# The column form of w by small TensorE products, with the issue order drawn up anew, in a fused linear-attention and feed-forward kernel

## The chip, the cores and the metric

One core of one Trainium2 chip. The metric is the device time of one execution in microseconds (us). Engines are named as the profile names them: PE is TensorE (PEld its weight loads), DVE is VectorE, ACT is ScalarE, POOL is GpSimd, SP is the queue of SyncE that issues most transfers. SBUF and PSUM are the two on-chip memories in which the kernel's tiles lie; the results of PE come into PSUM (`bank` in the profile). A *point* is 1% of the time of the kernel before.

## The reference, cut to what matters

```python
# r, k, v: (batch 4, heads 8, seq 768, head_dim 48); w, u: (8, 48)
state = zeros((B, H, D, D))
for t in range(S):
    cur = einsum('bhd,bhe->bhde', u * k[t], v[t])
    y[t] = einsum('bhd,bhde->bhe', r[t], state + cur)
    state = w[:, :, None] * state + einsum('bhd,bhe->bhde', k[t], v[t])
x = y.transpose(0, 2, 1, 3).reshape(3072, 384)
h = maximum(x @ w_in, 0)          # w_in  (384, 2048)
out = (h * h) @ w_out             # w_out (2048, 384)
```

The kernel works on 24 units, each 128 tokens of one batch. Inside a unit the recurrence becomes products of r and k with powers of w, a masked 128x128 product, and a state handed to the next unit of the same batch, which is scaled by w to the power 128. That last factor is wanted with the head dimension along the partitions: this is the "column form" of w.

## The kernel before

The kernel is a list of steps in one string, `ORDER`, and a table of functions, `Do`. A step such as `P0.10:D/0` says: product P0 of unit 10, on DVE, into buffer 0. The letter after the colon is the engine (A ACT, D DVE, G POOL, P PE, S the SP queue). Each engine runs its steps in the order of the string, so the string decides both which engine does a step and what stands ahead of it. The steps that matter here:

```python
def wc(e):                       # w as a column, by a transfer of single values
    for h in range(2):
        e.dma_start(out=wcol[64 * h : 64 * h + D, :], in_=w.rearrange("(a e) d -> e d a", e=2)[h])
def WLcol(e):                    # its 128th power
    e.activation(wcol, wcol, AF.Ln)
    e.activation(wcol, wcol, AF.Exp, scale=float(L))
def WLm(e): ...                  # spread to (128, 4, 96): factor of the state
def kh(e, i): e.tensor_mul(rk[..][:, 1, :, 0:D], loaded("k", i), early("WkP") if i < EARLY else Wkhat)
def rh(e, i): e.tensor_mul(rk[..][:, 0, :, 0:D], loaded("r", i), early("WtP") if i < EARLY else Wt2)
def P0(e, i): e.tensor_mul(P0b[..], loaded("r", i), loaded("k", i))
def P1(e, i): e.tensor_mul(t, t, ub)                       # t is P0b of the unit
def du(e, i): e.tensor_reduce(dub[..], P0b[..], axis=X, op=ALU.add)
def dv(e, i): e.tensor_mul(dvb[..], loaded("v", i), t)     # t is du, spread
def S(e, i):  e.tensor_mul(S0W[i % B], tsb[..], WLm)
# ... T, X: transposes by PE; Tc, xTc: their copies out of PSUM; XB, xX: the same by DMA
# ... A, Bm, Y, U, xs, ts: the attention; F1, re, sq, F2, os, out: the feed-forward part
# ... Z: PE products that nobody reads; cW: casts of weights; vb: cast of v
for step in ORDER.split():
    ...
    getattr(Do, name)(E[eng[0]], *at, *map(int, eng[1:]))
```

The six products kh, rh, P0, P1, dv and S have both inputs in SBUF (for the first four units kh and rh take one from PSUM). Each can run on DVE or on POOL, and the order says which, unit by unit.

## Time and profile before

| | before |
|---|---|
| time, median of 3 runs | 179.08 us (178.46 to 180.28) |
| span of the profiled execution | 178.6 us, mean granted clock 0.990 |
| PE, DVE, POOL busy | 166.0, 146.4, 58.8 us |
| PE idle (span less busy) | 12.6 us |

PE is the engine to watch: its idle time is the only thing that an order can win or lose, apart from the work itself. The groups of instructions by shape: here are three of VectorE's; the columns are line, engine, operation, tile and inputs, shapes, count, then busy us, mean ns of one, and idle time before them:

```profile
L342 DVE TENSOR_TENSOR P<-ldr,ldk 128x384 f32<-128x384 f32 x19 | 11.4, 606 | 0.0
L354 DVE TENSOR_TENSOR dv<-ldv,du 128x384 f32<-128x384 f32 x13 | 7.1, 550 | 0.0
L424 DVE TENSOR_TENSOR S0W<-ts,WLm 128x384 bf16<-128x384 f32 x11 | 6.6, 600 | 0.0
```

And two that have one input in PSUM (bank):

```profile
L411 DVE TENSOR_TENSOR xs<-bank,dv 128x384 bf16<-128x384 f32 x24 | 13.1, 551 | 2.1 <-POOL dv L354 1.8
L421 DVE TENSOR_TENSOR ts<-bank,S0W 128x384 f32<-128x384 f32 x16 | 8.8, 547 | 1.8 <-PE bank L403 1.8
```

The same shape, with both inputs in SBUF, takes 550 ns in one row and 606 in another. I use one sum for this all through the document, and call it **DVE's excess**: over all of DVE's TENSOR_TENSOR groups whose inputs are both in SBUF, count x (mean - 550 ns), with 415 ns in place of 550 for the bf16 squares (hq<-hr). For the kernel before it is 6.3 us.

### The profile page before, as it was taken

The numbers are of one execution on the slowest core, as the hardware profiler recorded it, in microseconds if no ns is written. First come the engines' busy times: TensorE is split into PE (matmuls) and PEld (weight loads), VectorE is DVE, ScalarE is ACT, GpSimd is POOL, SyncE is SP. The second block draws the span as 40 slices with busy tenths as digits, with TensorE's granted clock in tenths as the row PEclk, the third lists the DMA queues.
The fourth block names the chain that finished last, engine by engine and source line by source line (L and its number), as shares of the span: only waits on it lengthen the run. The fifth ranks groups of instructions, "written<-read, shape, count | busy, mean of one in ns | idle before, by whom it ended". The sixth has DMA issues, their size and how long they took to land.

```text
span 178.6 us, 4501 instructions
## 1 busy us (share of the span) xinstructions
PE 166.0 (93%) x1764; PEld 127.2 (71%) x1764; DVE 146.4 (82%) x294; ACT 108.6 (61%) x199; POOL 58.8 (33%) x70
## 2 busy tenths in 40 slices
PE   4986999989999979999989997999999999999992
PEld 4964987756788757776757665777768777877750
DVE  4999888595999999999999968999799659666420
ACT  2475875846597976978747655857835545332601
POOL 4084491036364533283377350292050000000000
PEclk9999699999999999999999999999999999999999
DMA  5998999989799999999999999997981200402122
GB/s 109 215 231 261 306 191 188 200 170 218 144 206 236 178 204 215 209 203 158 220 224 85 225 208 184 199 165 184 229 84 44 48 0 21 158 3 88 44 101 79
DMA packets 103749, 28.72 MB, mean 161 GB/s; under 512 B 96296, under 2 KB 103728, under 8 KB 103728
## 3 DMA queue, kind: packets, MB, share of 16 engines
q1 hardware_dynamic: 101688, 26.26, 73.9%
q0 software_dynamic: 1744, 1.77, 6.1%
q10 hardware_dynamic: 296, 0.40, 0.6%
q8 instruction: 14, 0.23, 0.5%
q14 instruction: 7, 0.06, 0.1%
HBM read 20.46 MB, written 4.72 MB: 141 GB/s over the span
## 4 chain that ended last, share of the span: by engine, by line
PE 42%; DVE 33%; DMA 14%; issue 5%; POOL 3%; ACT 1%; SPq 1%; DVEq 0%; POOLq 0%
PE bank L472 21%; PE bank L445 16%; DVE Bm L384 8%; DMA W<-in_moe_w_out_dram 6%; DMA wsa<-in_moe_w_in_dram 4%; DVE P L342 3%; DVE xs L411 3%; DVE du L349 3%; DVE rk L336 3%; DVE S0W L424 2%; DVE rk L339 2%; DVE ts L421 2%; DVE P L346 2%; DMA ldr<-in_r_dram 2%; POOL W L333 2%
## 5 line engine op out<-in xcount | busy, mean ns | idle before, releaser
L445 PE MATMUL bank<-xT,W 128*128 128x256 bf16 (+1 forms) x624 | 75.7, 268 | 1.8 <-DVE hq L462 1.1
L472 PE MATMUL bank<-W,hq 128*128 128x384 bf16 x384 | 72.0, 326 | 0.8 <-DMA W<-in_moe_w_out_dram 0.8
L445 PEld LDWEIGHTS <-W 128*128 128x128 bf16 x624 | 56.9, 100 | 13.1 <-issue 1.9
L453 ACT ACTIVATE hr<-bank 128x512 bf16<-128x512 f32 x76 | 44.4, 598 | 28.0 <-PE bank L445 27.2
L472 PEld LDWEIGHTS <-hq 128*128 128x128 bf16 x384 | 36.3, 98 | 19.6 <-issue 1.0
L460 ACT ACTIVATE hq<-hr 128x512 bf16<-128x512 bf16 x57 | 34.2, 628 | 4.4 <-DVE hr L455 4.2
L384 DVE TENSOR_TENSOR Bm<-bank,maskJT 128x512 bf16<-128x512 f32 x48 | 31.4, 681 | 2.2 <-PE bank L376 2.2
L260 ACT COPY os<-bank 128x384 f32<-128x384 f32 x18 | 8.6, 478 | 18.0 <-PE bank L472 16.0
L464 DVE TENSOR_TENSOR hq<-hr 128x512 bf16<-128x512 bf16 x37 | 15.3, 435 | 5.0 <-ACT hr L453 4.8
L455 DVE TENSOR_SCALAR hr<-bank 128x512 bf16<-128x512 f32 x20 | 13.8, 690 | 6.0 <-PE bank L445 4.5
L346 POOL TENSOR_TENSOR P<-P,ub 128x384 f32<-128x384 f32 x11 | 11.8, 1077 | 15.1 <-DVE P L342 15.0
L336 POOL TENSOR_TENSOR rk<-ldk,Wkhat 128x384 bf16<-128x384 f32 x9 | 10.8, 1205 | 13.2 <-DMA ldk<-in_k_dram 8.8
L354 POOL TENSOR_TENSOR dv<-ldv,du 128x384 f32<-128x384 f32 x11 | 9.1, 829 | 18.1 <-DVE du L349 15.0
L411 DVE TENSOR_TENSOR xs<-bank,dv 128x384 bf16<-128x384 f32 x24 | 13.1, 551 | 2.1 <-POOL dv L354 1.8
L394 PE MATMUL bank<-vb,Bm 128*128 128x48 bf16 x192 | 11.5, 184 | 2.4 <-DVE Bm L384 2.4
L349 DVE TENSOR_REDUCE du<-P 128x8 f32<-128x384 f32 x24 | 13.0, 542 | 0.1
L394 PEld LDWEIGHTS <-Bm 128*128 128x128 bf16 x192 | 9.6, 96 | 3.7 <-DVE Bm L384 2.3
L481 PE MATMUL bank<-identity 128*128 128x128 bf16 x101 | 9.7, 268 | 2.3 <-POOL identity masks.py:199 2.3
L342 DVE TENSOR_TENSOR P<-ldr,ldk 128x384 f32<-128x384 f32 x19 | 11.4, 606 | 0.0
L260 ACT COPY rkT<-bank 128x1024 bf16<-128x1024 bf16 x9 | 9.1, 1014 | 2.7 <-PE bank L363 2.6
L339 POOL TENSOR_TENSOR rk<-ldr,Wt 128x384 bf16<-128x384 f32 x6 | 7.1, 1183 | 9.6 <-DMA ldr<-in_r_dram 9.6
L481 PEld LDWEIGHTS <-identity 128*128 128x128 bf16 x101 | 8.3, 124 | 2.7 <-POOL identity masks.py:199 2.3
(62 smaller groups left out, 168.7 us busy)
## 6 DMA issues: line engine op xcount, KB each, us to landing
ldr<-in_r_dram SPq DMA_DIRECT2D x24, 192.0 KB, 3.8
ldk<-in_k_dram SPq DMA_DIRECT2D x24, 192.0 KB, 3.8
ldv<-in_v_dram SPq DMA_DIRECT2D x24, 192.0 KB, 3.9
out_dram<-os SPq DMA_DIRECT2D x22, 192.0 KB, 2.2
wsa<-in_moe_w_in_dram SPq DMA_DIRECT2D x7, 384.0 KB, 5.8
W<-in_moe_w_out_dram POOLq DMA_DIRECT2D x4, 384.0 KB, 8.8
out_dram<-os ACTq DMA_DIRECT2D x2, 192.0 KB, 1.9
rkT<-rk SPq DMA_TRANSPOSE x15, 3.7
```

Source lines behind the costliest of these rows:

```text
L260: e.copy(o, a)
L336: e.tensor_mul(rk[slot[f"rk{i}"]][:, 1, :, 0:D], loaded("k", i), early("WkP") if i < EARLY else Wkhat)
L342: e.tensor_mul(P0b[slot[f"P{i}"]], loaded("r", i), loaded("k", i))
L349: e.tensor_reduce(dub[slot[f"dv{i}"]], P0b[slot[f"P{i}"]], axis=mybir.AxisListType.X, op=ALU.add)
L384: e.tensor_mul(Bmb[slot[f"Bm{i}{h}"]], heads(bank(f"bA{i}{h}"), 128), mask_b)
L394: e.matmul(y[:, hc, D * h : D * (h + 1)], m[h][:, hc, :], vb[:, 2 * hc + h, :], start=(c == 0), stop=True, skip_group_check=True,)
L411: e.tensor_add(xsb[slot[f"xs{i}"]].rearrange("p (a b) -> p a b", a=HP), heads(bank(f"bY{i}"), 2 * D), dvb[slot[f"dv{i}"]].rearrange("p (a ...
L445: e.matmul(hp[:, fi, :], W1[f // 2][:, c, 128 * (f % 2) : 128 * (f % 2 + 1)], xt[:, c, :], start=(c == 0), stop=(c == CCH - 1), skip_group ...
L453: e.activation(hr, hp, AF.Relu)
L460: e.activation(hq, hr, AF.Square)
L472: e.matmul(bank(f"bO{i}", "bO")[:, 0:d_model], hqb[slot[f"hq{g},{f // m}"]][:, at : at + L], W2[q][:, f % 4, :], start=(f == 0), stop=(f = ...
L481: e.matmul(banks[b][:, 0:128], identity, identity, start=True, stop=True, skip_group_check=True)
```

## The change

Its intent: the two transfers of 4-byte values, which lie on a full DMA queue, go; eight PE products of one row by a 1x1 one turn the row of w, which is already in SBUF, into the column; and the issue order is drawn up anew around this.

```diff
-    nc.vector.memset(wcol, 1.0)
+    one = const.tile([1, 1], FP32, name="one")
+    nc.vector.memset(one, 1.0)
...
         def wc(e):
-            for h in range(2):
-                e.dma_start(out=wcol[64 * h : 64 * h + D, :], in_=w.rearrange("(a e) d -> e d a", e=2)[h])
+            for h in range(H):
+                p0 = 64 * (h % 2)
+                e.matmul(
+                    bank("bW")[p0 : p0 + D, h // 2 : h // 2 + 1], wb[0:1, h, :], one,
+                    start=True, stop=True, skip_group_check=True,
+                )
 
         def WLcol(e):
-            e.activation(wcol, wcol, AF.Ln)
-            e.activation(wcol, wcol, AF.Exp, scale=float(L))
+            for p0 in (0, 64):
+                e.activation(wcol[p0 : p0 + D, :], bank("bW")[p0 : p0 + D, 0:HP], AF.Ln)
+                e.activation(wcol[p0 : p0 + D, :], wcol[p0 : p0 + D, :], AF.Exp, scale=float(L))
...
 ORDER = """     (all lines replaced; two of them, with products that changed engine)
-Y.8:P/2 P1.10:D ... rh.11:D X.9:P/3 ... S.7:D sq.4.3:A0/25 ... S.6:D os.5:A/0
+P0.10:G/1 F1.4.0:P/0 ... rh.11:G re.4.3:A/3 ... S.6:G ... P1.10:G ... S.7:G
```

For units 4 and later, 63 of the steps P0, P1, kh, rh, dv, S and vb changed engine, in both directions. Of the 51 products with both inputs in SBUF that POOL now does for these units, 33 were DVE's before; of the 41 that it did before, 23 went to DVE.

## The prediction

> **What bounds the kernel now.** I first read the page's busy shares and its slices, to find the regimes.
>
> ```profile
> PE 166.0 (93%) x1764; PEld 127.2 (71%) x1764; DVE 146.4 (82%) x294; ACT 108.6 (61%) x199; POOL 58.8 (33%) x70
> ...
> PEclk9999699999999999999999999999999999999999
> DMA  5998999989799999999999999997981200402122
> ```
>
> TensorE (PE) is busy 93% of 178.6 us, the sixteen DMA engines are full until about 125 us, and the granted TensorE clock dips in one slice near 20 us. Next came a table of stretches (columns: stretch, length, busy time and count of PE, PEld, DVE, ACT, POOL, granted clock, DMA share, GB/s), to see which engine is full where:
>
> ```profile
> 16.00:18.00 2.00, 1.00 (x24) 0.75 (x22) 2.00 (x4) 0.85 (x2) 0.54 (x1) 1.00 0.93 283
> 18.00:20.00 2.00, 1.83 (x22) 1.66 (x20) 1.90 (x5) 1.42 (x2) 0.00 (x0) 0.60 1.16 317
> 20.00:22.00 2.00, 2.00 (x23) 2.00 (x22) 1.49 (x4) 1.86 (x5) 1.61 (x2) 0.55 1.14 289
> ...
> 60.00:80.00 20.00, 18.87 (x216) 14.38 (x215) 19.97 (x36) 15.89 (x31) 9.87 (x10) 1.00 1.02 207
> 80.00:100.00 20.00, 19.32 (x204) 13.91 (x202) 19.89 (x39) 13.09 (x26) 11.25 (x11) 1.00 1.20 178
> ...
> 100.00:120.00 20.00, 18.52 (x199) 13.74 (x198) 17.50 (x35) 13.67 (x27) 7.83 (x8) 1.00 1.02 198
> 120.00:140.00 20.00, 20.00 (x219) 15.22 (x217) 18.77 (x39) 11.70 (x22) 4.07 (x5) 1.00 0.63 122
> ```
>
> There are four regimes. Until 18.6 us PE waits for data and does little that counts. From there to 37 us it is nearly always busy, and waits for the second weight matrix at the end. From 44 to about 104 us VectorE (DVE) has no idle time and PE only little. From 110 us PE alone sets the end. The chain of waits in order of time, and the timeline, show the joints:
>
> ```profile
> 13.58 6.73 DMA wsa<-in_moe_w_in_dram
> 20.36 0.81 POOL W L262
> ...
> 25.25 0.69 POOL W L333
> 25.95 11.37 DMA W<-in_moe_w_out_dram
> ...
> 167.91 7.16 PE bank L472 x44
> 175.09 0.48 ACT os L260
> ```
>
> The reader should see that the transfer of column w is nowhere in it: the chain passes from the weights' loads through the POOL queue to the last load of w_out. What the transfer cost is in the view of its tile:
>
> ```profile
> L305 SPq DMA_DIRECT2D wcol<-in_w_dram x2: 438/462/486, 20.3 to 20.8; - x2
> L314 POOL COPY WLm<-wcol x2: 337/343/349, 28.1 to 28.5; 48x192 f32<-48x192 f32 x2
> ...
>   POOL WLm L314: 1.4, 1
> ...
>   DVE S0W L418: 0.3, 1
> ...
> DMA to landing us min/median/max: 4.4/4.4/4.4
> ```
>
> Two issues of 0.46 us on the SP queue, landing 4.4 us later; POOL waited 1.4 us and DVE 0.3 us for what is made of it.
>
> My budget of PE time: the span is 18.6 us until the first product with w_in, then work to 175.1, then 3.5 us of last copy and store. PE's gaps after 25 us, summed from the table of stretches, are 0.2 (25 to 30) + 0.8 (35 to 40) + 1.1 + 0.7 + 1.5 (60 to 120) = 4.3 us. Clock: 0.40 x 2.0 + 0.45 x 2.0 = 1.7 us of PE's full-clock time is withheld between 18 and 22 us. So if everything else stayed, no order of issue could win more than about 6 us, and a 2% gain (3.6 us) needs more than half of that.
>
> **What the Trainium skill says.** "TensorE: Matmul & The Clock Gate", section "What's actually happening": the gate opens after a busy window of some 3.4 us and falls to half rate after an idle one. The trace agrees in size (0.55 to 0.60 over 18 to 22 us, after a stretch with PE busy 1.00 of 2.00 us), though PE was not wholly idle before it. "DMA: Bandwidth & Descriptors", section "Specifications": under 512 B a transfer is not at line rate; the page's DMA line has 96296 of 103749 packets under 512 B, and the engines are full at some 200 GB/s. The 4-byte values of w are the extreme of that, but there are only 2 x 48 x 4 = 384 of them, 0.4% of the packets. "SBUF — State Buffer", section "Who interferes with whom": a VectorE instruction with two SBUF inputs contends with a GpSimd one that reads SBUF. The trace agrees: the product for rk from r takes 548 ns on DVE while its factor is in PSUM (4 early ones) and 629 ns with both in SBUF (14 later ones).
>
> **The change, part by part.** (a) Removed: two SP issues (0.97 us of SP time), 384 packets. At 73.9% of 16 engines' 178.6 us for 101688 packets a packet costs some 21 ns of one engine, so an estimate of 384 x 21 / 16 = 0.5 us of the DMA's time in the full stretch. Worth 0 to 0.5 us.
>
> (b) Added: eight products of one row by one column, 48 results each, after the first unit's transposes, where PE has filler work anyway; an estimate of 8 x 0.1 to 0.2 us = 0.8 to 1.6 us there if each is split in several passes, none of it on the later path. ScalarE runs four small functions rather than two, 4 x 0.2 = 0.8 us, before 12 us, where it has gaps. WLm is then ready on POOL near 19 us rather than 28.85. The state products S0 follow at once, but DVE lost only 0.3 us there.
>
> (c) The start. ScalarE now loads its table (1.28 us) before it issues the load of the row of w, rather than after. In the trace the issue begins at 1.37 and the data land 2.99 us later; it will now begin near 2.2, so every step made from w shifts by some 0.8 us. Against that stand weights: w_in's first slice is the 14th load on SP in both orders behind the same bytes (ten loads of r, k, v, two slices), landed at 17.6 us, and must be cast (0.9 us). I count the new DVE order from the shuffle to the second unit's xs: some 24 instructions of about 0.5 us, which gives the first w_in product 18.6 to 19.4 rather than 18.6. A loss of 0 to 0.8 us.
>
> (d) Fillers. Z products go from 101 to 127: 61 rather than 50 at the start, then 66 rather than 51 between the early steps, with 25 and 18 placed in the gaps of 11 to 17 us. I take it that the dip at 18 to 22 us goes, or mostly: 0 to 1.7 us won, which more than pays for (c).
>
> (e) POOL's queue. W.1.3, the last w_out load, was issued at 26.0 us after a cast (0.82 us) among the issues. That cast moves to DVE, and WLm's copies come ahead. By the POOL order the five issues start near 21.0 rather than 22.0 and end near 24.7. Those loads share full DMA engines, so I credit 0.5 to 1 us of landing, 36.5 rather than 37.35.
>
> (f) Moves between engines, counted from the two orders, each at the mean of its row in the groups by shape. Off DVE: 5 P0 (606), 3 S (600), 3 dv (550), 4 os (554), 6 rh (629), 3 squares in bf16 (435), 3 vb (349) = 3.0 + 1.8 + 1.7 + 2.2 + 3.8 + 1.3 + 1.0 = 14.8 us. Onto DVE: 2 P1 (666), 3 kh (675), 2 re (690), 2 squares from PSUM (680), 3 Tc (no DVE row; an estimate of 0.9 us from 357 ns for 384 columns), 2 casts of weights (estimate 0.7 from 349 ns for half), 3 xTc (357) = 1.3 + 2.0 + 1.4 + 1.4 + 2.7 + 1.4 + 1.1 = 11.3 us. DVE has 3.5 us less, near 143. POOL gets 10 us more (5 P0, 6 rh, 3 S, 3 dv; less 3 kh, 2 P1, 2 casts, 1 vb), near 69, and will lengthen DVE's two-input instructions by an estimated 1 us. Of the 2.5 us net, PE can gain at most what it idles for want of DVE, part of the 3.3 us between 60 and 120: say 1 us.
>
> (g) Two more units transposed by PE rather than by DMA: 6 products of 0.11 us = 0.7 us on PE, which is the bound. Two DMA transposes less lie on the full SP queue.
>
> Sum, middle values: (a) -0.2, (b) 0, (c) +0.4, (d) -0.9, (e) -0.5, (f) -1.0, (g) +0.7 = -1.5 us. (d) and (e) overlap, since PE that runs ahead then waits for w_out. From 179.1 that is 177.6.
>
> **The rivals.** First, the transfer was hidden and nothing takes its place: the SP queue and DMA are full with other loads, PE goes on at 93%, gaps move about. For: the chain of waits leaves wcol out. That gives 178.5 to 179.5. Second, a new wait: GpSimd takes rh, P0, S and dv at 0.8 to 1.2 us each, some double of DVE's, and these stand ahead of transposes and xs; if POOL is late, DVE and PE wait, as already at 106.3 us, where xs waited 1.8 us for dv on POOL. Against: POOL is at 33%. That would give 180 to 182. Third, the late w: unit 0 and 1 come late, F1 starts at 20 us and the clock still falls: 179.5 to 181. Fourth, all gains arrive and the new order also closes half the gaps of 60 to 120 us: 175 to 176.
>
> **Range and chances.** I give my sum 50%, the first rival 22%, the second and third together 15%, the fourth 13%. Median 177.6 us, 175.5 to 180.0 eight times in ten. 2% faster means below 175.5 us, where only the fourth gets to: 0.12. 2% slower means above 182.7: 0.04.
>
> **What would show it.** Right: the clock above 0.9 in 18 to 22 us; the shuffle of w near 5.3 us rather than 4.5; WLm done near 20 us; the last w_out load landed before 37 us; DVE near 143, POOL near 69; w_in's first product at 18.6 to 19.4 us; PE full from 110 us on. Wrong: the clock falls again, PE's gaps after 25 us add up to over 5 us, or waits of DVE for POOL over 2 us each. A result below 175 would mean that gaps of DVE and PE were closed that I left standing; one above 181, that POOL or the late row of w set a new bound.

## The result, and the profile after

| | before, same rounds | after |
|---|---|---|
| time, median | 178.77 us (178.22 to 180.28) | 188.81 us (187.92 to 189.6) |
| ratio of the fast runs, 95% interval | | 1.0546 (1.0464 to 1.0628) |
| span of the profiled execution | 178.6 us | 187.2 us |
| PE busy, idle | 166.0, 12.6 us | 168.1, 19.1 us |
| DVE's excess | 6.3 us | 17.9 us |

A ratio is the mean time of one kernel's fast runs over the mean of the other's fast runs in the same rounds, so it is not quite the ratio of the two medians.

The change is slower by 5.5%. The prediction of 177.6 us, with its range to 180.0, was wrong. The page of the kernel after:

```profile
PE 168.1 (90%) x1812; PEld 127.9 (68%) x1812; DVE 154.2 (82%) x284; ACT 108.5 (58%) x204; POOL 70.9 (38%) x79
...
PEclk9999999999988999999999999999999999999999
```

DVE does ten instructions fewer and is busy 7.8 us longer. The dip of the granted clock at 20 us is gone, but there is one two slices wide at 51 to 61 us. In the table of stretches of the kernel after (columns: stretch, length, busy time and count of PE, PEld, DVE, ACT, POOL, clock, DMA share, GB/s):

```profile
18.00:20.00 2.00, 2.00 (x43) 1.90 (x39) 1.73 (x4) 1.65 (x4) 1.88 (x5) 1.00 0.89 274
20.00:22.00 2.00, 2.00 (x46) 1.93 (x43) 2.00 (x5) 2.00 (x4) 2.00 (x4) 1.00 0.98 299
50.00:60.00 10.00, 7.23 (x74) 4.94 (x73) 8.58 (x15) 5.12 (x11) 3.12 (x3) 0.83 1.05 166
80.00:100.00 20.00, 17.50 (x198) 13.14 (x195) 19.22 (x32) 11.68 (x24) 8.86 (x9) 1.00 0.72 151
100.00:120.00 20.00, 18.26 (x193) 13.74 (x188) 19.80 (x34) 13.45 (x28) 11.31 (x11) 1.00 0.86 177
120.00:140.00 20.00, 18.38 (x207) 13.89 (x205) 19.27 (x35) 12.77 (x25) 9.75 (x9) 1.00 0.71 145
```

and the one row of the same view of the kernel before that the prediction left out:

```profile
50.00:60.00 10.00, 10.00 (x126) 8.16 (x123) 9.97 (x20) 8.90 (x18) 5.05 (x6) 1.00 1.03 205
```

The loss stands in these rows. PE idles 2.77 + 2.50 + 1.74 + 1.62 = 8.6 us in 50 to 60 and 80 to 140 us; before it was 0 + 0.68 + 1.48 + 0 = 2.2 us. The difference of 6.4 us is as much as the whole growth of PE's idle time (19.1 - 12.6 = 6.5); what else changed, 1.8 us more from 22 to 25 us and less in other stretches, cancels out. In the remaining 2.1 us of the span PE is busy longer. It does 48 instructions more (26 products Z, 16 for w and 6 transposes), but that these are the 2.1 us is not shown: runs told below with the same 1812 instructions were busy between 163.8 and 168.1 us. In 100 to 140 us DVE is busy 39.1 of 40 us and still does fewer instructions than before (69 rather than 74). So DVE's instructions have become longer. And it is DVE that PE waits for. Of the 8.6 us, 8.4 end with an instruction of DVE by the view of waits, and none with one of POOL; here are those of 50 to 60 and of 80 to 100 us (who waited for whom, us, times, longest):

```profile
PE bank L382 <- DVE rkT L263: 1.5, 1, 1.5
PE bank L382 <- DVE ts L427: 1.2, 1, 1.2
...
PE bank L398 <- DVE Bm L390: 1.8, 1, 1.8
PE bank L409 <- DVE Bm L390: 0.7, 1, 0.7
```

The groups by shape of the kernel after, to be laid beside those of before:

```profile
L348 DVE TENSOR_TENSOR P<-ldr,ldk 128x384 f32<-128x384 f32 x14 | 11.3, 810 | 0.0
L360 DVE TENSOR_TENSOR dv<-ldv,du 128x384 f32<-128x384 f32 x10 | 7.9, 792 | 0.0
L430 DVE TENSOR_TENSOR S0W<-ts,WLm 128x384 bf16<-128x384 f32 x8 | 7.7, 963 | 0.0
...
L417 DVE TENSOR_TENSOR xs<-bank,dv 128x384 bf16<-128x384 f32 x24 | 13.0, 550 | 2.0 <-PE bank L400 1.7 <-POOL dv L360 0.3
L427 DVE TENSOR_TENSOR ts<-bank,S0W 128x384 f32<-128x384 f32 x16 | 8.7, 546 | 0.4 <-POOL S0W L430 0.4
```

606 to 810, 550 to 792 and 600 to 963 ns, for the same operation on the same shapes. The last two rows, with one input in PSUM, kept their length (551 to 550 and 547 to 546 ns). Instruction by instruction the trace says the same. In the kernel after, 40 of DVE's 103 two-input instructions overlap in time with a product, cast or copy of POOL, and they hold all of the excess, 17.9 us, some 0.45 us each and at most 0.83; the other 63 hold 0.0. In the kernel before it is 27 of 118 with 6.3 us, some 0.23 each, and 91 with 0.0. The timeline of the kernel after shows where the first gap comes from (columns: start, length, engine, line, operation, tile and inputs, count, and in brackets the idle time before it and what ended it):

```profile
46.04 2.44 POOL L342 TENSOR_TENSOR rk<-ldk,Wkhat 128x384 bf16<-128x384 f32 x2 [0.91 <-PE bank L400]
...
47.55 2.62 DVE L348 TENSOR_TENSOR P<-ldr,ldk 128x384 f32<-128x384 f32 x2
...
48.44 1.31 POOL L345 TENSOR_TENSOR rk<-ldr,Wt 128x384 bf16<-128x384 f32 x1
...
49.71 1.31 POOL L348 TENSOR_TENSOR P<-ldr,ldk 128x384 f32<-128x384 f32 x1
50.09 1.35 DVE L352 TENSOR_TENSOR P<-P,ub 128x384 f32<-128x384 f32 x1
...
52.54 0.38 PE L382 MATMUL bank<-rkT 48*128 48x128 bf16 x7 [1.23 <-DVE ts L427]
...
53.74 0.68 DVE L263 COPY rkT<-bank 128x1024 bf16<-128x1024 bf16 x1
...
54.47 0.61 PE L382 MATMUL bank<-rkT 48*128 48x128 bf16 x8 [1.55 <-DVE rkT L263]
```

From 47.55 to 51.44 us DVE does three products, which would take 3 x 0.55 = 1.65 us, and needs 3.89, while POOL works through four of its own without a pause, from 46.04 to 51.02 us. The copy rkT, which PE waits for, stands behind them in DVE's queue, and behind one more product that took 0.94 us. PE works 0.61 us in the 3.38 us from 51.09 to 54.47, and then the clock falls (0.50 over 54.4 to 57.6 us).

The two things that the change was about were harmless. The products for w (first row: eight of them, in two passes each) and what ACT makes of them lie at 8.6 to 10.5 us, and POOL spreads the result at 18.1 us rather than 28.1:

```profile
8.64 0.52 PE L307 MATMUL bank<-one,wb 1*48 1x1 f32 x16
...
9.66 0.17 ACT L314 ACTIVATE wcol<-bank 48x4 f32<-48x4 f32 x1
...
L320 POOL COPY WLm<-wcol x2: 343/344/345, 18.1 to 18.5; 48x192 f32<-48x192 f32 x2
```

**The theory** from this: POOL now does more products that read SBUF, they collide with DVE's products with two SBUF inputs, and DVE, which had no time to spare from 44 to 104 us even in the kernel before, passes the loss to PE. The overlaps above show the first half; that the time comes from there is for experiments to show. **Its rivals**: the column of w itself; the products being twice as long on POOL, so that those who wait for them wait longer (no collision needed); and the new order standing badly in some other way.

### The profile page after: what moved, and what is told of

Its sections match the earlier page's. It is cut to its first block, busy times and chain, and to the rows that moved or that the text cites. A ratio compares the mean times of both kernels' runs of the same rounds, so it can differ in the third digit from the quotient of the medians.

```text
span 187.2 us, 4588 instructions
## 1 busy us (share of the span) xinstructions
PE 168.1 (90%) x1812; PEld 127.9 (68%) x1812; DVE 154.2 (82%) x284; ACT 108.5 (58%) x204; POOL 70.9 (38%) x79
## 5 line engine op out<-in xcount | busy, mean ns | idle before, releaser
L451 PE MATMUL bank<-xT,W 128*128 128x256 bf16 (+1 forms) x624 | 75.4, 266 | 2.8 <-DVE W L263 1.8
L261 ACT COPY os<-bank 128x384 f32<-128x384 f32 x22 | 10.5, 478 | 20.7 <-PE bank L478 20.6
L360 POOL TENSOR_TENSOR dv<-ldv,du 128x384 f32<-128x384 f32 x14 | 13.0, 928 | 18.8 <-DVE du L355 18.7
L430 POOL TENSOR_TENSOR S0W<-ts,WLm 128x384 bf16<-128x384 f32 x8 | 8.9, 1116 | 19.6 <-DVE ts L427 19.6
L348 POOL TENSOR_TENSOR P<-ldr,ldk 128x384 f32<-128x384 f32 x10 | 11.7, 1182 | 11.6 <-DMA ldr<-in_r_dram 11.6
L382 PE MATMUL bank<-rkT 48*128 48x128 bf16 x192 | 9.7, 221 | 6.4 <-DVE ts L427 2.0
L352 POOL TENSOR_TENSOR P<-P,ub 128x384 f32<-128x384 f32 x9 | 10.0, 1108 | 14.2 <-DVE P L348 14.2
L345 POOL TENSOR_TENSOR rk<-ldr,Wt 128x384 bf16<-128x384 f32 x12 | 13.8, 1156 | 3.8 <-DMA ldr<-in_r_dram 3.8
L382 PEld LDWEIGHTS <-rkT 48*128 48x128 bf16 x192 | 6.0, 95 | 10.7 <-issue 7.1
L342 POOL TENSOR_TENSOR rk<-ldk,Wkhat 128x384 bf16<-128x384 f32 x6 | 7.0, 1173 | 13.8 <-DMA ldk<-in_k_dram 12.9
L398 PE MATMUL bank<-S0W,rkT 128*128 128x96 bf16 x80 | 9.8, 204 | 2.1 <-DVE Bm L390 2.1
```

The source lines that it names most:

```text
L345: e.tensor_mul(rk[slot[f"rk{i}"]][:, 0, :, 0:D], loaded("r", i), early("WtP") if i < EARLY else Wt2)
L360: e.tensor_mul(dvb[slot[f"dv{i}"]], loaded("v", i), t)
L382: e.matmul(heads(bank(f"bA{i}{h}"), 128)[:, hc, :], t[p0 : p0 + D, HP + hc, :], t[p0 : p0 + D, hc, :], start=True, stop=True, skip_group_c ...
L451: e.matmul(hp[:, fi, :], W1[f // 2][:, c, 128 * (f % 2) : 128 * (f % 2 + 1)], xt[:, c, :], start=(c == 0), stop=(c == CCH - 1), skip_group ...
```

## The experiments

Ratios are to the kernel before in the same rounds, three rounds each. The medians of before in these rounds lay between 179.91 and 180.76 us, a little above the 178.77 of the first rounds; so compare ratios, not medians.

### The two halves of the change, each alone

wc_only: the order of before, with the column made by PE.

```diff
-... T.1:P/0 du.1:D/0 ... lW.0.3:S/2 ... wc:S ... re.2.5:D/0 WLcol:A
+... T.1:P/0 wc:P/0 du.1:D/0 ... Tc.0:A/1 WLcol:A ...
```

> The old issue order with the column of w made by eight small TensorE products (two passes each) instead of the transfer; everything else stays. If the small products cost nothing on the path that sets the end, as the profile of the changed kernel suggests (0.52 us of PE near 8.6 us), this is the time before within 0.5%: 178 to 179.5 us. If the column form by TensorE itself carried the loss of 8 to 10 us, this would be near 188 us.

order_only: the order of after, with the column brought by the transfer.

```diff
-... T.0:P/0 rh.1:D ld.v.1:S/1 wc:P/1 ... Z.2.5:P WLcol:A
+... lW.0.3:S/2 wc:S ... re.0.2:A/4 WLcol:A ... W.1.3:G WLm:G
```

> The new issue order with the old transfer of single values for w, WLm made after the last load of w_out as in the kernel before. If the loss lies in the new order and the new split of work between engines, this stays near the changed kernel: 187 to 190 us. If the small products were to blame, it falls to near 179 us.

Measured: wc_only 180.55 us, ratio 1.0015 (0.9942 to 1.0087). order_only 187.12 us, ratio 1.0399 (1.0321 to 1.0476), with an excess of 16.6 us. The column by PE costs nothing that can be seen by itself, and the new order alone brings most of the loss. The excess of wc_only was 8.6 us, though its DVE has the same work in the same order as in the kernel before (6.3): some 2 us of excess come and go without a change of time. Between order_only and the full change lie 1.5 points; their intervals hardly touch, and no run here says what they are.

### The division of products between DVE and POOL, exchanged

after_old_split: the order of after, but the 63 steps go to the engines they had before. before_new_split: the order of before, with the engines of after.

```diff
 # after_old_split, some of the 63
-P0.8:G/3 P0.10:G/1 S.6:G dv.9:G rh.11:G kh.11:D/4 P1.11:D
+P0.8:D/3 P0.10:D/1 S.6:D dv.9:D rh.11:D kh.11:G/4 P1.11:G
```

> The changed kernel, its issue order untouched, but for units 4 and later each of the steps P0, P1, kh, rh, dv, S and vb goes back to the engine that had it before (63 steps change engine). Theory of contention (more GpSimd work that reads SBUF blocks VectorE's two-input instructions): VectorE's busy time falls by 5 us or more, the excess of its two-input SBUF instructions over 550 ns falls from 18 us to under 10 us, and the time to 180 to 184 us. Theory of order (the queues wait on each other whatever the split): the time stays at 186 to 190 us.

> The counterpart: the kernel before, its issue order untouched, with the new kernel's engines for the same steps of units 4 and later. Theory of contention: the time rises by 4 us or more, to 183 to 189 us, and VectorE's P, dv and S instructions take 700 ns and more on the mean. Theory of order: within 2 us of 179.

Measured: after_old_split 186.84 us, ratio 1.0374 (1.0286 to 1.0463), excess 11.1 us. before_new_split 186.54 us, ratio 1.0348 (1.0280 to 1.0416), excess 14.3 us, POOL busy 68.3 us. The division alone makes the old order 3.5% slower, nothing else being changed in it: that speaks for the division of work, and all of its excess lies on instructions that overlap with reads of POOL. But going back to the old division in the new order wins only 1.7 points, where I had expected far more. These two runs can't tell a collision from a step that merely waits longer for another engine, so one of them is taken up again below.

### More work on POOL that nobody waits for

before_pool_reads: the kernel before with ten useless POOL products from SBUF, 1.13 us on the mean, put into POOL's order from unit 4 on. before_pool_writes: ten memsets of 1.02 us in the same places, which write and do not read.

```diff
+        def J(e, n):
+            e.tensor_mul(junk, wb, ub)      # before_pool_writes: e.memset(junkb, 0.0)
-... P1.5:G F2.3.0:P/1 ... dv.7:G ld.r.10:S/3 ...
+... P1.5:G J.0:G F2.3.0:P/1 ... dv.7:G J.1:G ld.r.10:S/3 ...
```

> The kernel before, with ten useless GpSimd products (two SBUF operands, 128x384, about 1.05 us each, the amount by which the change raised GpSimd's busy time) spread between 45 and 130 us; nobody reads their result. Theory of contention: VectorE's excess over 550 ns rises by 4 us or more and the time by 2 to 5 us. Theory that only the late results of the moved steps hurt (latency of GpSimd): within 1 us of before, as nothing was moved.

> The control: ten GpSimd memsets of about the same duration at the same places, which read nothing. Theory of contention: VectorE's excess stays at 6 to 8 us and the time within 1 us of before. If mere occupation of GpSimd (steps behind it come later) is what counts, it rises as much as with the products.

Measured: before_pool_reads 180.98 us, ratio 1.0029 (0.9964 to 1.0093), excess 11.0 us, POOL busy 69.9 us. before_pool_writes 179.51 us, excess 9.4 us; two of its four runs were slow, and its ratio of 0.988 (0.978 to 0.998) is unclear. Expected were 2 to 5 us for the reads, and that was missed: the excess rose by 4.7 us and the time by 0.3% (interval -0.4 to +0.9%). This was the run that spoke most against the theory. POOL may be as busy as in the kernel after (70.9 us) and the excess nearly double, without a loss that can be seen. Perhaps these collisions fell where PE had work in hand; that is not shown. The memsets were expected to leave the excess at 6 to 8 us, and that was missed as well. The trace settles why: 34 instructions that overlap with POOL's real products, casts or copies hold all of it, and the one that lies beside a memset alone is not longer. So what rose are collisions with the real products, whose places the memsets had shifted.

### The reads taken out, the work left in place

The direct test. In after_no_reads every POOL product of units 4 and later becomes a product of one column (128x1), a memset of the same output and a second memset, 1.09 us together on the mean (a real one in the kernel after: 1.12). Order, engines and POOL's load stay; the large reads are gone. The results are wrong on purpose. before_no_reads is the same edit on the kernel before. Since the first small product releases its inputs early, after_no_reads_held adds a second one at the end, which holds them as long as the real product does. In both of these the output is written by the second piece, so that a step waiting for it goes on some 0.5 us too early; after_no_reads_late makes the memset of the output the last of the four pieces. They were to take 1.3 us and took 1.13 on the mean.

```diff
+    def mul(e, i, o, a, b, a1, b1):
+        if e is nc.gpsimd and i >= EARLY:
+            e.tensor_mul(junk, a1, b1)      # 128x1
+            e.memset(o, 0.01)
+            e.memset(junkb, 0.0)
+            # after_no_reads_held: e.tensor_mul(junk, a1, b1) once more
+            # after_no_reads_late: tensor_mul, memset(junkb), tensor_mul, memset(o)
+        else:
+            e.tensor_mul(o, a, b)
```

> The changed kernel, wrong on purpose: every GpSimd product of units 4 and later becomes a product of one value per partition (it keeps the wait for the operands) and two memsets of about the same length in all, so GpSimd stays as busy but reads almost nothing. Theory of contention: VectorE's excess falls from 18 us to under 4 us and the time from 188 to 178 to 182 us. Theory of order: the time stays above 185 us.

> The same surgery on the kernel before, wrong on purpose. Its excess is 6 us, so contention gives at most 1 to 3 us: 176 to 178.5 us. If the two kernels come out equal without reads, contention is the whole difference; if the changed one stays 4 us or more behind, the order has its own part.

> As the changed kernel without reads, wrong on purpose, but each step ends with a second product of one value per partition, so its operands' buffers are given up only when the real product would have given them up, and it lasts about 1.1 us. If the 14 us won without reads are really contention, this stays at 173 to 177 us. If they came from loads that could start earlier because buffers were free at once, it goes back to 182 us or more.

> As after_no_reads_held (operands held to the end), but the memset of the output is the last of the four pieces, so that a step that waits for the product is released no earlier than by a real one (about 1.3 us in all, a real product takes 1.0 to 1.2 us alone). If collisions of reads are the cause, the time stays at 174 to 176 us (ratio 0.965 to 0.98) with an excess near 0. If earlier release of the waiting steps had made the gain of the two earlier runs, the time returns to 180 us or more.

| | median us | ratio, 95% interval | DVE's excess | POOL busy | DVE busy |
|---|---|---|---|---|---|
| after | 188.81 | 1.0546 (1.0464 to 1.0628) | 17.9 | 70.9 | 154.2 |
| after_no_reads | 173.99 | 0.9653 (0.9591 to 0.9716) | 0.0 | 69.0 | 136.9 |
| after_no_reads_held | 174.78 | 0.9690 (0.9620 to 0.9760) | 0.0 | 75.4 | 137.4 |
| after_no_reads_late | 175.78 | 0.9725 (0.9651 to 0.9799) | 0.1 | 70.8 | 137.1 |
| before_no_reads | 179.26 | 0.9941 (0.9859 to 1.0023) | 1.6 | 58.5 | 141.9 |

The rows of after_no_reads that answer to those above, and its row of PE in 40 slices:

```profile
L261 DVE TENSOR_TENSOR P<-ldr,ldk 128x384 f32<-128x384 f32 x14 | 7.6, 547 | 0.0
L261 DVE TENSOR_TENSOR dv<-ldv,du 128x384 f32<-128x384 f32 x10 | 5.5, 548 | 0.0
L261 DVE TENSOR_TENSOR S0W<-ts,WLm 128x384 bf16<-128x384 f32 x8 | 4.4, 548 | 0.0
...
PE   4998959999999999999999999999999999999991
```

Each product is back at 547 or 548 ns, and PE is full from 26 us to the end. The new order goes from 5.5% slower to 3.5% faster, with POOL as busy as in the kernel after: POOL's load does not explain the loss, since it stayed. The early release of the inputs doesn't either, since the held form keeps 3.1 of the 3.5%, nor an early output, since the late form keeps 2.7. This takes away the second rival too: in the late form a step waits as long for POOL's piece (1.13 us) as for a real product (1.12). I had expected 178 to 182 us of after_no_reads, so the gain is larger than I thought. In the old order the same edit wins 0.6%, with an interval that takes in no gain at all, where I had expected 1 to 3 us; that its excess of 6.3 us lay where it did little harm fits this, but isn't shown. The same run answers the objection that wrong numbers might be quicker to compute: it is as wrong, and not clearly faster. And without the reads the new order with its own division is the better one, by some 5 us: 173.99 against 179.26 us.

after_old_split_no_reads is the same edit, in its late form, on the new order with the old division, the run that had missed its expectation:

> The new order with the old division of products (1.037 with reads, excess 11.0 us), and the reads of GpSimd's products of units 4 and later taken out as in after_no_reads_late. If collisions made its loss too, the time falls to 174 to 178 us (ratio below 0.99). If its loss is the mismatch of order and division, which makes steps wait for engines whatever they collide with, it stays above 183 us (ratio above 1.015).

Measured: 178.88 us, ratio 0.9867 (0.9765 to 0.9970), excess 0.1 us. One of its four runs was marked slow (the ratio is of the three others), and the verdict against the kernel before is unclear. With the reads the ratio was 1.0374, and these two intervals lie far apart. So collisions made this kernel's loss too, five points of it, though their sum was only 11.1 us. Between it and after_no_reads_late remain 1.4 points with intervals that overlap; DVE has 5.3 us more work in it (142.4 us busy, not 137.1), so what the order's fit to its division is worth is not told apart. before_new_split was not run without reads.

### Which of the reads it is

after_moved_no_reads takes the reads from the 33 products that were DVE's before; after_stay_no_reads from the 18 that were POOL's already; both in the form of after_no_reads.

```diff
-        if e is nc.gpsimd and i >= EARLY:
+        if e is nc.gpsimd and step_name in BARE:    # the 33, or the 18
```

> The changed kernel, wrong on purpose: only the 33 steps of units 4 and later that the change moved from VectorE to GpSimd lose their reads; the 18 that GpSimd had before, too, are real. If the moved steps are what costs, nearly all of the loss to the kernel before is won back: 176 to 181 us, VectorE's excess 4 to 8 us.

> The complement, wrong on purpose: the 18 steps that GpSimd had before lose their reads, the 33 moved ones are real. If contention grows with the number of colliding reads, a third of the gain is left: 182 to 186 us, excess 9 to 13 us.

Measured: after_moved_no_reads 178.33 us, ratio 0.9890 (0.9811 to 0.9970), excess 3.8 us. after_stay_no_reads 181.61 us, ratio 1.0074 (0.9988 to 1.0160), excess 9.1 us. The moved ones bring 6.6 of the 8.9 points, the others 4.7; together more than the whole. So it isn't only that POOL got more: taking away reads that POOL had all along helps as well, in the new order. Either part alone leaves little of the loss, +0.7% with the 33 and -1.1% with the 18; the full loss takes both.

### A correct kernel with fewer reads on POOL

after_rebalanced: the full change, and 16 late products P0 and S from POOL to DVE, paid for with 8 relus from DVE to ACT. after_rebalanced_tc: two copies Tc from DVE to ACT as well, among them the one that PE waited for at 54 us. after_rebalanced_more: in addition 7 products rh from POOL to DVE and 12 squares from DVE to ACT. All three give the right result.

```diff
 # after_rebalanced (some)
-P0.8:G/3 S.6:G S.7:G P0.13:G/4 P0.15:G/3 re.3.7:D/2 re.4.5:D/0
+P0.8:D/3 S.6:D S.7:D P0.13:D/4 P0.15:D/3 re.3.7:A/2 re.4.5:A/0
 # after_rebalanced_tc
-Tc.4:D/4 Tc.7:D/0
+Tc.4:A/4 Tc.7:A/0
 # after_rebalanced_more (some)
-rh.8:G rh.9:G rh.10:G sq.4.4:D2/28 sq.5.2:D2/7
+rh.8:D rh.9:D rh.10:D sq.4.4:A0/28 sq.5.2:A0/7
```

> A try at a use: the changed kernel, correct, with 8 of VectorE's relu steps moved to ScalarE and GpSimd's 16 late P0 and S steps moved to VectorE. Contention: excess 8 to 12 us rather than 18, time 180 to 185 us. If ScalarE becomes late with the relus, TensorE waits for banks and it stays near 188 us.

> The rebalanced version still took 1.012 of the kernel before, with a gap of 2 us of TensorE at 50 to 60 us, where its transposes' consumer waited 1.55 us for VectorE's copy of rkT of unit 7, and the clock granted there was 0.83. Here the copies Tc of units 4 and 7 go to ScalarE, nothing else. If the rest of the loss is that copy's place behind colliding products, TensorE loses less than 0.7 us in 50 to 60 us, the clock stays above 0.95 there and the time is about 180 us (ratio 0.995 to 1.005). If the rest is collisions elsewhere, the gap may go but the ratio stays at 1.008 to 1.015.

> As the one before, and in addition 12 squares of groups 3 to 9 from VectorE to ScalarE and 7 rh products of units 8 to 17 from GpSimd to VectorE. If contention is what is left, VectorE's excess falls from about 10 us to 7 us or less, GpSimd's busy time to about 48 us, and the time is 178 to 180 us, no slower than the kernel before. If VectorE's own work is the bound instead, taking seven products more costs what it saves and the time stays at 180 to 182 us; if ScalarE becomes the bound it is over 182 us.

| | median us | ratio, 95% interval | DVE's excess | POOL busy | ACT busy |
|---|---|---|---|---|---|
| after_rebalanced | 182.22 | 1.0115 (1.0052 to 1.0179) | 9.8 | 55.2 | 112.4 |
| after_rebalanced_tc | 180.73 | 1.0039 (0.9960 to 1.0118) | 9.8 | 55.4 | 114.1 |
| after_rebalanced_more | 178.53 | 0.9907 (0.9839 to 0.9976) | 4.5 | 45.1 | 119.9 |

The row of 50 to 60 us in the table of stretches, of after_rebalanced:

```profile
50.00:60.00 10.00, 8.03 (x90) 5.79 (x88) 8.99 (x18) 5.60 (x12) 2.55 (x3) 0.83 1.15 197
```

of after_rebalanced_tc:

```profile
50.00:60.00 10.00, 8.62 (x107) 6.64 (x106) 10.00 (x19) 8.59 (x17) 4.42 (x4) 1.00 1.11 218
```

and of after_rebalanced_more, with its busy line:

```profile
50.00:60.00 10.00, 9.37 (x114) 7.19 (x113) 10.00 (x20) 9.20 (x18) 1.72 (x2) 1.00 0.51 101
...
PE 164.5 (93%) x1812; PEld 126.4 (72%) x1812; DVE 142.3 (81%) x285; ACT 119.9 (68%) x226; POOL 45.1 (26%) x56
```

Most of the loss comes back with 16 products. Moving the two copies closes part of the gap (1.97 to 1.38 us; I had named 0.7) and brings the clock from 0.83 to 1.00 in this stretch, for 0.8 points, as far as the two ratios, from different rounds with intervals that overlap, can tell. In after_rebalanced_more DVE is busy 6.7 us less than in after_rebalanced. The moved work explains some 2.6 of them (12 squares of 0.42 us and 2 copies of 0.68 less, 7 products of 0.55 more); the fall of the excess, by 5.3 us, is the larger part, and the two together say more than was seen, by about 1 us. The full change is then faster than the kernel before by 0.9%. That is the best ratio of the correct kernels, but a small gain: at 2% it counts as the same time.

## Why the prediction was wrong

(f), the moves between engines, is the step that failed, and in one term: POOL's added products "will lengthen DVE's two-input instructions by an estimated 1 us". They lengthened them by 17.9 - 6.3 = 11.6 us, and with these reads taken out the loss was gone (0.9653 in place of 1.0546). The rest of (f) was well counted. It expected DVE's own work to shrink by 3.5 us; without the excess it went from 146.4 - 6.3 = 140.1 to 154.2 - 17.9 = 136.3 us, 3.8 less. POOL was expected at 69 us and came to 70.9. So the balance for DVE was -3.8 + 11.6 = +7.8 us where the prediction had -2.5, on an engine that had no idle time from 44 to 104 us and was already the one that PE waits for. From the same mistake comes the next sentence of (f), that PE can only gain part of its 3.3 us: it took the gaps as something that can only shrink.

The mechanism was in the prediction, with 548 against 629 ns as its evidence. The 1 us was given without a sum. A sum over DVE's groups would have shown 6.3 us of excess in the kernel before, beside 49.5 us of POOL's products from SBUF. But scaling that up doesn't help much: these products grew to 64.6 us, by 1.3, and the excess by 2.8. How much collides depends on which instructions of the two engines stand beside one another (27 of 118 before, 40 of 103 after, and at twice the loss each), and the order was new throughout. The prediction also counted only net moves, 12 products to POOL, where, from unit 4 on, 33 went there and 23 came back. The honest reading would have been a far wider range upward.

The second rival, "a new wait: GpSimd takes rh, P0, S and dv", named the right steps at 180 to 182 us, and set against it that POOL is at 33%. That is the wrong measure: POOL was late for hardly anyone. DVE waited for its products 0.9 us in all (S0W 0.4, dv 0.3, P 0.2), and in the kernel before 1.8 us for dv alone. POOL was in DVE's way while it worked, and after_no_reads shows it at the same busy time without the harm. The prediction's own line for the case of a result above 181 us, that POOL or the late row of w set a new bound, was half right: it was POOL, but as what DVE collides with, and not as a bound of its own.

(a) and (b), the transfer and the products of w: right. wc_only, at 1.0015, is their measure. The eight products begin at 8.64 us and take 0.52 us rather than the 0.8 to 1.6 of the estimate.

(c), the start: wrong in a harmless way. The issue of the load of the row of w starts at 1.37 us in both kernels, and the shuffle at 4.36 rather than at 4.49 us. The table load, at 0.80 to 2.08 us, runs beside the issue. The first product with w_in comes at 18.46 us rather than between 18.6 and 19.4.

(d), the fillers: right for its place. The clock is 1.00 from 18 to 22 us. But the same 17% of ten microseconds, 1.7 us, is withheld from 50 to 60 us instead, after the first of the new gaps.

(e), POOL's queue: right so far as the issues go: they begin at 20.1 us and are done near 24, and no wait for w_out is left among PE's products that read it. The half microsecond can't be seen in the sum, for PE waits 1.8 us for a cast of w_in at 24.8 us, which itself waited for its load.

(g), two more units transposed by PE: the counts agree (6 more of such instructions among the 48), the cost is not told apart within the 2.1 us by which PE is busy longer.

What would show it wrong, said the prediction: "PE's gaps after 25 us add up to over 5 us". They add up to 9.8 us over 25 to 160 us. That was the right thing to look at. Nor was PE full from 110 us on, as expected: from 120 to 140 us it idled 1.6 us.

What stays open: why nearly equal excess costs so unequal time. An excess of 11.0 us went with 1.003 in before_pool_reads and one of 11.1 with 1.037 in after_old_split, 9.8 with 1.012 in after_rebalanced. The runs show that the collisions are the cause in the new order, with either division, not a rule for their price. What was seen at 51 to 54 us is a collision that costs because PE has no work in hand behind it; that this is the rule is not shown.

## What to carry to other kernels

Where POOL shares the elementwise products with DVE, count DVE's two-input time as it is measured in the trace against the shortest of the same shape, and treat a move of a product to POOL as costing DVE time as well as saving it: here each of them gave DVE some 0.55 us and could take up to 0.8 from the product beside it. If a schedule is to be trusted, let it know of the collision, or move work to an engine that doesn't collide: giving relus, squares and two copies to ACT and taking products back from POOL brought 6 points. And to separate a collision from a load or a wait, take the reads out and leave the time in: that one wrong kernel settled what the six correct ones before it did not.

## What the Trainium skill lacked or had wrong

- "SBUF — State Buffer", section "Who interferes with whom": its rule held wherever it was tested (excess 17.9 us with POOL's reads, 0.0 with memsets of the same length in place of them; none on DVE's products with one input in PSUM). What it lacks is a measured size for this pair. A 128x384 fp32 product of DVE took 547 to 550 ns alone and up to 1374 ns (a state product) beside a POOL product; the mean of a row rose from 550 to 792 or from 600 to 963 ns. POOL's own product of this shape took 1.00 us in the clear and often 1.31 us in a collision. Nor does the page say that the loss can't be read off the busy shares: at 70 us of POOL time the excess was 17.9, 11.0 or 0.0 us.
- "TensorE: Matmul & The Clock Gate", section "What's actually happening", has the clock fall after an idle window. Here it fell after 3.38 us in which PE had worked for 0.61 us, in spread pieces, so a window need not be wholly idle; the page does not say how much work it may hold.
- "ScalarE: Activation LUTs", section "What ACT_TABLE_LOAD costs": its 1283 ns are the 1.28 us of the trace. It doesn't say that a transfer issued from the same queue after the load doesn't wait for it: the issue began at 1.37 us, inside the load at 0.80 to 2.08 us, and (c) of the prediction rested on the opposite.
